# The second channel product with seven block products instead of eight

## The chip, the cores and the metric

The kernel runs on one NeuronCore of a Trainium2 chip. The metric is the device time of one execution in microseconds (us). The engines are named as the profile names them: PE is TensorE's matmuls and PEld its weight loads, DVE is VectorE, ACT ScalarE, POOL GpSimd, SP SyncE, which only issues DMAs here.

## The reference

Attention over selected blocks of keys, and then one token-mixing and one channel-mixing layer, for 4 batches of 768 tokens with 8 heads of 64 (512 channels).

```python
def _attn_ref(q, k, v):                       # (4, 8, 768, 64) each
    k_rep = k.reshape(B, H, n_blocks, block, D).mean(axis=3)      # blocks of 64
    gate_scores = np.einsum('bhsd,bhnd->bhsn', q, k_rep)
    ...                                       # causal blocks only
    top_idx = np.argsort(gate_scores, axis=-1)[..., -top_k:]      # top_k = 3
    ...                                       # mask: chosen blocks and own block, causal
    scores = np.where(mask, scale * np.matmul(q, k.transpose(0, 1, 3, 2)), -1000000000.0)
    attn = np.exp(scores - np.max(scores, axis=-1, keepdims=True))
    attn = attn / (np.sum(attn, axis=-1, keepdims=True) + 1e-09)
    return np.matmul(attn, v).astype(np.float32)

def _moe_ref(x, w_tok1, w_tok2, w_ch1, w_ch2):                    # x (4, 768, 512)
    xt = x.transpose(0, 2, 1)
    h = np.maximum(xt @ w_tok1, 0.0) @ w_tok2                     # 768 -> 256 -> 768
    u = x + h.transpose(0, 2, 1)
    h2 = np.maximum(u @ w_ch1, 0.0) @ w_ch2                       # 512 -> 1536 -> 512
    return (u + h2).astype(np.float32)
```

The change concerns the last product, relu(u @ w_ch1) @ w_ch2, for each batch a 768 x 1536 matrix by a 1536 x 512 one.

## The kernel before

All matmuls take 16-bit operands, except the transposes of q and k and the gate scores, and add up in 32-bit PSUM. The work is made of small operations, each with an engine, an estimated cost, dependencies, a priority and the buffers that it takes. A planner (`plan`, line 68) walks through them with the estimated costs: on each engine it takes, of what could start within 60 ns of the earliest, the one with the lowest priority number. The order so found is then issued as it stands (line 886), and each engine works through its own list in that order. A wait of one instruction on an engine therefore holds all that stands behind it on that engine.

The attention goes over 16 pairs of heads (four per batch): transposes of k and q (L359), their copies to SBUF on ScalarE (L368) and casts to 16 bits on GpSimd (L374), the gate scores (`gate`, L400), the choice of blocks on VectorE (`gm`, `top`, `below`, `bias`), the mask turned by TensorE (`mask`, L443) and put under q by VectorE (`put_mask`, L451), the scores (L465), the exponential on ScalarE (L478), the diagonal on VectorE (`diag`, L485, a product of two 16-bit SBUF tensors), the product with v (L496), and its normalization into `x16` (L515). Pair i has priorities around 10 i.

The mixing of batch b follows: `tok1`, `relu1`, `umix`, `uadd` make u. For batch 0, u is transposed on TensorE (`utr`, `uput`); for the others it is stored to DRAM and read back transposed by two DMAs of SP (`store_u` L344, `turn_u` L350). Then `ch1` (L608) makes 12 chunks of 128 hidden channels for 768 tokens, in pieces of 512 and 256 tokens, with `relu2` on ScalarE (L618, 512 tokens) and VectorE (L620, 256 tokens) into `h2`, which has the hidden channels on the partitions. `ch2` (L629) takes one of six row tiles j of 128 tokens: 12 matmuls of 512 columns with a chunk of `h2` as weights and a chunk of `wc2_16` as the moving operand, in three parts of four matmuls that the planner places separately. `oadd` (L637) adds u, and `store` (L641) sends 128 x 512 results of 32 bits. The last row tile of the last batch is cut into 320 and 192 columns. These have priorities from 1000 (b + 1) on, so that TensorE takes them where the attention leaves it free.

PSUM has eight banks: two "big" tiles of two banks (transposes and scores), one "av" tile for L496, and three "bank" tiles for all the rest. RINGS (L209) gives the number of buffers of each kind. Constants are loaded and buffers cleared ahead of the planned part (L852 to L884), among them `blk` on GpSimd's queue (L883), which serves a second way of preparing k for pairs from VIA (16) on. The weights of the mixing come by GpSimd's queue as casting DMAs, placed behind certain casts of the attention (WAIT, L38); those of `wc2_16` are the last four.

Of the kernel before, what the change touches and what calls it, by code (L numbers as in the profile page):

```python
# [32 lines left out]
VIA = 16  # L33
# [21 lines left out]
class Buf:  # L55


    __slots__ = ("ring", "users", "slot")

    def __init__(self, ring):  # L60
        self.ring, self.users, self.slot = ring, [], None
# [6 lines left out]
def plan(ops, rings, near=60.0):  # L68
# [31 lines left out]
    left = len(ops)  # L100
    while left:
# [7 lines left out]
        for e, cand in ready.items():  # L109
            if not cand:  # L110
                continue
            lst = []
            if e == "SP":
                if any(x.eng == e and x.prio < min(c.prio for c in cand) for x in ops if id(x) not in done):
                    continue
                cand = [min(cand, key=lambda c: c.prio)]
            for op in cand:
                t = free[e]
                for d in op.deps:
                    t = max(t, finish(d, e))  # L120
                ok = True
                for buf in op.takes:
                    first = None
                    for s, (_, old) in enumerate(slots[buf.ring]):
                        f = 0.0 if old is None else buf_free(old, e)
                        if f is not None and (first is None or f < first[0]):
                            first = (f, s)
                    if first is None:
                        ok = False
                        break  # L130
                    t = max(t, first[0])
                    buf.slot = first[1]
                if ok:
                    lst.append((t, op))
            if not lst:
                continue
            t0 = min(t for t, _ in lst)
            pick = min((x for x in lst if x[0] <= t0 + near), key=lambda x: (x[1].prio, x[0]))
            if best is None or pick[0] < best[0]:
                best = pick  # L140
        assert best is not None, "the plan cannot go on"
        t, op = best
        op.start = t
        for buf in op.takes:
            slots[buf.ring][buf.slot] = (0.0, buf)
# [32 lines left out]
def kernel(  # L178
# [31 lines left out]
                 x16=3, h1=2, u=2, uT=2, h2=1, ob=3)  # L210
# [14 lines left out]

    V16 = [sp.tile([128, 2, NJ, 65], F16, tag=f"V{r}", name=f"V{r}") for r in range(R + 1)]
# [3 lines left out]
    K16 = [sp.tile([96, 8, 256], F16, tag=f"K16{y}", name=f"K16{y}") for y in range(2)]  # L230
    ks2 = [sp.tile([128, 2 * NB], FP, tag=f"ks{r}", name=f"ks{r}") for r in range(R)]
    bn16 = [sp.tile([128, NJ, 2, 64], F16, tag=f"bn{r}", name=f"bn{r}") for r in range(R)]
# [3 lines left out]
    wc2_16 = sp.tile([128, NFC, DM], F16, tag="wc2", name="wc2")  # L236
    warm = sp.tile([128, 256], F16, tag="warm", name="warm")
# [46 lines left out]
    def load_k8(i):  # L284
        b, h = pairs[i]

        def f():
            t = sb("kt", [128, 2, 8, D], FP, f"k8_{i}")[0:96]
            T["k8", i] = t
            nc.sync.dma_start(out=t.rearrange("p g t d -> p g (t d)"),  # L290
                              in_=k[b, h:h + 2].rearrange("g (p t) d -> p g (t d)", t=8))
        return f

    def ksum8(i):
        def f():
            t = sp.tile([96, 2, D], FP, tag="kp", bufs=2, name=f"kp_{i}")
            T["kp", i] = t
            nc.vector.tensor_reduce(out=t, in_=T["k8", i].rearrange("p g t d -> p g d t"), axis=AX.X, op=ALU.add)
        return f

    def ksum_pe(i):
        def f():
            p = ps("bank", [128, NB], "kps")
            T["kst", i] = p
            nc.tensor.matmul(out=p, lhsT=T["kp", i].rearrange("p g d -> p (g d)"), rhs=blk, start=True, stop=True)
        return f

    def cast_k8(i):
        def f():
            y = i % 2  # L310
            nc.gpsimd.tensor_copy(out=K16[y].rearrange("p t (g c) -> p g t c", g=4)[:, 0:4:3, :, :], in_=T["k8", i])
        return f

    def store_k(i):
        def f():
            t = dram.tile([S, 256], F16, tag=f"ks{i % 2}", name=f"kscr_{i}")
            T["kscr", i] = t
            nc.sync.dma_start(out=t.rearrange("(p t) c -> p (t c)", t=8), in_=K16[i % 2].rearrange("p t c -> p (t c)"))
        return f

    def turn_k(i):
        return lambda: nc.sync.dma_start_transpose(out=KAX[:, i % R, :, :], in_=T["kscr", i])

    def k16_zero(y):
        return lambda: nc.gpsimd.memset(K16[y].bitcast(FP), 0.0)

    def k16_ind(y):
        def f():
            for c in (64, 128):
                nc.gpsimd.tensor_copy(out=K16[y][:, :, c:c + NB],  # L330
                                      in_=blk.rearrange("p (o n) -> p o n", o=1).broadcast_to([96, 8, NB]))
        return f

# [28 lines left out]
    def evac_t(t32, i):  # L362
        def f():
            name = "qt" if t32 == "ql" else "kt"
            t = sb(name, [128, S if name == "qt" else 1024], FP, f"{name}_{i}")[:, 0:S]
            T[name, i] = t
            p = T["tr", t32, i]
            nc.scalar.copy(out=t, in_=p[:, 0:S])  # L368
        return f
# [60 lines left out]
    def bias(i):  # L430
        def f():
            nc.vector.scalar_tensor_tensor(
                out=bn16[i % R][:, 1:NJ, :, 0:NB],
# [4 lines left out]
    def mask(i):  # L438
        def f():
            p = ps("bank", [128, 128 * GJ], "bps", F16)  # L440
            T["bps", i] = p
            for j in range(GJ):
                nc.tensor.transpose(out=p[:, 128 * j:128 * j + 128],  # L443
                                    in_=bn16[i % R][:, j + 1, :, :].rearrange("p x n -> p (x n)"),
# [157 lines left out]
    def ch1(b, fc, n):  # L602
        def f():
            a, e = CH[n]
            p = ps("bank", [128, e - a], "c1")
# [18 lines left out]
    def ch2(b, j, part, lo, hi):  # L624
# [6 lines left out]
        return f  # L631

# [35 lines left out]
    for i in range(NP):  # L668
# [7 lines left out]

        if i >= VIA:
            kb = Buf("kt")
            ld = op("SP", 500, 0, [], pre - 12, load_k8(i), [kb], size=1400)
            O["ksum", i] = dve(1100, [ld], pre + 1, ksum8(i))  # L680
            nb = Buf("bank")
            O["kpe", i] = pe(115, [O["ksum", i]], pre + 1, ksum_pe(i), [nb])
            O["kcopy", i] = dve(260, [O["kpe", i], O.get(("gate", old))], pre + 1, kcopy(i))
            nb.users.append(O["kcopy", i])
            y = i % 2
            if i < VIA + 2:
                O["kz", y] = op("POOL", 1100, 1150, [], pre - 1, k16_zero(y))
                O["ki", y] = op("POOL", 400, 450, [O["kz", y]], pre - 1, k16_ind(y))
            O["castk", i] = op("POOL", 1150, 1200, [ld, O["ki", y], O.get(("kst", i - 2))], pre + 3, cast_k8(i))
            kb.users += [O["ksum", i], O["castk", i]]  # L690
            O["kst", i] = op("SPO", 600, 0, [O["castk", i], O.get(("cast", "kt", i, 0))], pre + 3.1, store_k(i), size=1600)
            O["kturn", i] = op("SPO", 600, 0, [O["kst", i]] + last_scores(0) + last_scores(1), pre + 3.2, turn_k(i), size=2500)
            O["cast", "kt", i, 0] = O["cast", "kt", i, 1] = O["kturn", i]
        zq = [op("POOL", 880, 930, [], pre - 1, zero_q(i))] if 0 < i < R else []
        for t32, src, off in (("kl", k, 0), ("ql", q, 0.1))[i >= VIA:]:
# [37 lines left out]
        O["bias", i] = dve(195, [O["lt", i], O.get(("mask", old))], pre + 3, bias(i))  # L733
# [33 lines left out]
    for n, (at, f) in enumerate(wq):  # L767
        W.append(op("POOL", 700, 0, [O[("cast",) + WAIT[n]]], at, f, size=3200 if n < 2 else 2100))

    for b in range(B):  # L770
# [46 lines left out]
        for fc in range(NFC):  # L817
            for n in range(2):
                bk = Buf("bank")
                O["ch1", b, fc, n] = pe((864, 436)[n], ([O["uturn", b]] if b >= UVIA else [O["uput", b, cc] for cc in range(NCC)]) + W[2:6],  # L820
                                        fill + 20 + 2 * fc + n, ch1(b, fc, n), [bk])
# [8 lines left out]
        for j in range(NJ):  # L830
            cuts = ((0, DM),) if b < B - 1 or j < NJ - 1 else ((0, 320), (320, DM))
            for lo, hi in cuts:
                bk = Buf("bank")
                prev = None
                for part in range(3):
                    dp = [O["relu2", b, fc, n] for fc in range(NFC) for n in range(2)] + W[6:10] if prev is None else [prev]
                    prev = pe(4 * (2.5 + (hi - lo) / 2.4), dp, fill + 50 + 3 * j + part + lo / 1000, ch2(b, j, part, lo, hi),
                              [bk] if part == 0 else [])
                    h2b.users.append(prev)
                ob = Buf("ob")  # L840
                o = dve(70 + 1.04 * (hi - lo), [prev], early, oadd(b, j, lo, hi), [ob])
                bk.users.append(o)
                ub.users.append(o)
                s = op("SPO", 600, 0, [o], early, store(b, j, lo, hi), size=2 * (hi - lo))
                ob.users.append(s)
# [5 lines left out]
    with tc.manual_schedule():  # L851
# [23 lines left out]
        for r in range(R):  # L875
# [7 lines left out]
        blk = const("blk", (np.arange(96)[:, None] // 8 == nidx[None, :]).astype(np.float32), FP, nc.gpsimd)  # L883
# [37 lines left out]
```

## Time and profile before

| | us |
|---|---|
| device time, median of 3 runs | 273.73 (272.89 to 274.72) |
| span of the profiled execution, first to last instruction | 270.4 |
| median less that span | 3.3 |
| TensorE busy (97%) | 262.6 |
| VectorE busy (60%) | 161.0 |
| ScalarE busy (53%) | 142.6 |
| GpSimd busy (30%) | 81.5 |

The profiled execution's own time is its span and what lies around it (start and end of the program), which the table's third row gives by way of the median. Matmuls are pipelined, and their recorded durations (379 ns for 512 columns) contain the way through the array. The pace at which they follow each other is read from the chain of waits, where a block of n matmuls is shown with its whole length. "Idle before" in a group's line is time in which the engine stood still ahead of such instructions, and an arrow names what ended it.

| stage | from, to (us) |
|---|---|
| attention, with mixing of batch 0, `ch1` of batch 0, u of batch 1, `ch2` of batch 0 as filler | 12 to 163 |
| batch 1: `ch1`, with u of batch 2 | 163 to 183 |
| batch 1: `ch2` | 183 to 199 |
| batch 2: `ch1`, with u of batch 3; `ch2` | 199 to 236 |
| batch 3: `ch1` | 236 to 251 |
| batch 3: `ch2`, last matmul at 266.7 | 251 to 267 |

### The profile page before, as it was taken

To read this page: it belongs to the slowest core of one execution; us is meant where nothing else is said; L and a number is where in the kernel's file an instruction comes from. 1 tells how busy PE (TensorE), PEld (TensorE's weight loads), DVE (VectorE), ACT (ScalarE), POOL (GpSimd) and SP (SyncE) were. 2 spreads that over 40 slices of the span, in tenths; PEclk is the share of its full clock that TensorE was granted. 3 is DMA by queue.
4 is the path that set the end of the run, shared out by engine and by line. 5 is a ranking of instruction groups with operands and counts; after the bars stand their busy time and mean duration, and the time that the engine had idled before them with its cause. 6 is when DMAs were issued, how large, how long until landed. Compare 5 with 4: busy or idle time off the path is not lost.

```text
span 270.4 us, 5927 instructions
## 1 busy us (share of the span) xinstructions
PE 262.6 (97%) x2309; PEld 174.5 (65%) x2309; DVE 161.0 (60%) x561; ACT 142.6 (53%) x188; POOL 81.5 (30%) x112
## 2 busy tenths in 40 slices
PE   8899999999999999999999999999999999999994
PEld 5787588877787877776876655544455544465443
DVE  4558968997979777879888533334233252333222
ACT  2367997777888898788487704430024400044100
POOL 8688816763465365336432000000000000000000
PEclk9999999999999999999999999999999999999999
DMA  8999999999999985480741121003920017510032
GB/s 173 205 212 224 189 215 214 197 200 200 213 209 228 212 176 133 103 174 3 158 117 41 39 77 42 0 2 116 260 89 2 0 48 196 153 72 0 2 135 97
DMA packets 94411, 34.67 MB, mean 128 GB/s; under 512 B 85616, under 2 KB 90888, under 8 KB 94384
## 3 DMA queue, kind: packets, MB, share of 16 engines
q1 hardware_dynamic: 90272, 29.89, 50.5%
q0 software_dynamic: 3392, 4.15, 9.1%
q8 instruction: 18, 0.29, 0.5%
q10 hardware_dynamic: 720, 0.25, 0.5%
q14 instruction: 9, 0.07, 0.1%
HBM read 27.21 MB, written 8.65 MB: 133 GB/s over the span
## 4 chain that ended last, share of the span: by engine, by line
PE 87%; DMA 4%; DVE 4%; ACT 3%; issue 1%; SPq 1%; DVEq 0%; ACTq 0%
PE c L629 23%; PE c L608 23%; PE sps L465 12%; PE aps L496 7%; PE gps L400 5%; DMA ql<-in_q_dram 4%; PE tql L359 4%; PE ups L539 3%; PE tkl L359 3%; PE tok L527 3%; ACT e L478 3%; PE bps L443 2%; PE warm L648 1%; PE tok L558 1%; DVE Q L451 1%
## 5 line engine op out<-in xcount | busy, mean ns | idle before, releaser
L478 ACT ACTIVATE e<-sps 128x1024 f16<-128x1024 f32 (+1 forms) x96 | 84.6, 918 | 16.9 <-PE sps L465 12.0
L608 PE MATMUL c<-uT,wc 128*128 128x256 f16 (+1 forms) x384 | 68.1, 326 | 0.2 <-ACT h L618 0.2
L618 ACT ACTIVATE h<-c 128x512 f16<-128x512 f32 x48 | 28.7, 598 | 69.0 <-PE c L608 61.7
L629 PE MATMUL c<-wc,h 128*128 128x512 f16 (+2 forms) x300 | 64.9, 370 | 0.0
L608 PEld LDWEIGHTS <-wc 128*128 128x128 f16 x384 | 37.1, 98 | 24.5 <-issue 0.4
L465 PE MATMUL sps<-Q,KA 128*128 128x512 f16 (+3 forms) x256 | 50.1, 305 | 1.0 <-ACT e L478 0.7
L629 PEld LDWEIGHTS <-h 128*128 128x128 f16 x300 | 28.8, 98 | 31.3 <-issue 0.6
L620 DVE TENSOR_SCALAR h<-c 128x256 f16<-128x256 f32 x48 | 20.2, 420 | 33.8 <-PE c L608 33.8
L637 DVE TENSOR_TENSOR ob<-u,c 128x512 f32<-128x512 f16 (+2 forms) x25 | 16.6, 666 | 38.4 <-PE c L629 38.4
L485 DVE TENSOR_TENSOR e<-e,m 128x256 f16<-128x256 f16 x90 | 31.1, 353 | 12.9 <-ACT e L478 12.2
L374 POOL CAST KA<-kt 64x768 f16<-64x768 f32 x32 | 27.0, 845 | 27.4 <-ACT kt L368 24.2
L465 PEld LDWEIGHTS <-KA 128*128 128x128 f16 x256 | 22.4, 100 | 15.2 <-issue 1.2
L374 POOL CAST Q<-qt 64x768 f16<-64x768 f32 x32 | 26.9, 841 | 10.8 <-ACT qt L368 9.3
L496 PE MATMUL aps<-V,e 128*128 128x65 f16 x672 | 27.0, 193 | 0.1
L496 PEld LDWEIGHTS <-e 128*128 128x128 f16 x672 | 25.6, 98 | 2.2 <-issue 0.4
L400 PEld LDWEIGHTS gps<-ks,qt 128*128 128x128 f32 x160 | 19.2, 192 | 2.4 <-DVE ks L390 1.3
L280 POOL CAST V<-v 128x768 f16<-128x768 f32 x16 | 13.3, 832 | 24.0 <-DMA v<-in_v_dram 19.8
L400 PE MATMUL gps<-ks,qt 128*128 128x24 f32 x160 | 20.0, 267 | 0.3 <-DVE ks L390 0.2
L368 ACT COPY kt<-tkl 128x768 f32<-128x768 f32 x16 | 12.8, 799 | 11.7 <-PE tkl L359 5.9
L515 DVE TENSOR_TENSOR x<-aps,rc 128x384 f16<-128x384 f32 x32 | 17.6, 550 | 0.5
L451 DVE COPY Q<-bps 12x640 f16<-12x640 f16 x32 | 15.5, 484 | 1.9 <-PE bps L443 0.8
L368 ACT COPY qt<-tql 128x768 f32<-128x768 f32 x16 | 12.8, 798 | 6.5 <-PE tql L359 5.7
(55 smaller groups left out, 218.0 us busy)
## 6 DMA issues: line engine op xcount, KB each, us to landing
kl<-in_k_dram SPq DMA_DIRECT2D x32, 192.0 KB, 4.8
ql<-in_q_dram SPq DMA_DIRECT2D x32, 192.0 KB, 4.6
v<-in_v_dram SPq DMA_DIRECT2D x16, 384.0 KB, 5.4
out_dram<-ob SPq DMA_DIRECT2D x23, 256.0 KB, 2.0
wc<-in_moe_w_ch_dram POOLq DMA_DIRECT2D x8, 384.0 KB, 7.4
uscr<-u SPq DMA_DIRECT2D x3, 768.0 KB, 3.7
w<-in_moe_w_tok_dram POOLq DMA_DIRECT2D x2, 384.0 KB, 6.8
out_dram<-ob SPq DMA_DIRECT2D x1, 160.0 KB, 1.8
```

The lines of the kernel that those rows point to most:

```text
L359: nc.tensor.transpose(out=p[:, 128 * j:128 * j + 128], in_=t[:, j, :], identity=ident32)
L368: nc.scalar.copy(out=t, in_=p[:, 0:S])
L374: nc.gpsimd.tensor_copy(out=dst[i % R][x][lo:lo + 64, :], in_=T[name, i][lo:lo + 64, :])
L400: nc.tensor.matmul(out=g[:, j, :], lhsT=T["qt", i][:, 128 * j + 128:128 * j + 256], rhs=ks2[i % R], start=True, stop=True)
L465: nc.tensor.matmul(out=p[:, off + a:off + a + n], lhsT=KA[i % R][x][:, 128 * kk:128 * kk + 128], rhs=QA[i % R][x][:, q0 + a:q0 + a + n], s ...
L478: nc.scalar.activation(out=e[:, 0:width], in_=T["sps", i, x, g][:, 0:width], func=AF.Exp, scale=scale)
L485: nc.vector.tensor_tensor(out=d, in0=d, in1=m0, op=ALU.mult)
L496: nc.tensor.matmul(out=p[:, jq, :], lhsT=T["e", i, x, g][:, o:o + 128], rhs=V16[i % (R + 1)][:, x, kk, :], start=(kk == 0), stop=(kk == jq))
L608: nc.tensor.matmul(out=p, lhsT=wc1_16[:, cc, 128 * fc:128 * fc + 128], rhs=T["uT", b][:, cc, a:e], start=(cc == 0), stop=(cc == NCC - 1))
L618: nc.scalar.activation(out=T["h2", b][:, fc, a:e], in_=T["c1", b, fc, n], func=AF.Relu)
L620: nc.vector.tensor_scalar(out=T["h2", b][:, fc, a:e], in0=T["c1", b, fc, n], scalar1=0.0, scalar2=None, op0=ALU.max)
L629: nc.tensor.matmul(out=T["c2", b, j, lo], lhsT=T["h2", b][:, fc, 128 * j:128 * j + 128], rhs=wc2_16[:, fc, lo:hi], start=(fc == 0), stop=( ...
```

## The change

`ch2`, `oadd` and `store` are no longer used. The product of each pair of row tiles (j, j + 3) with `wc2_16` is written as a 2 x 2 block product: the hidden channels are halved (chunks 0 to 5 and 6 to 11), and so are the 512 output columns. One level of Strassen's method, in Winograd's arrangement, then takes seven products of 128 x 768 by 768 x 256 in place of eight, each of six matmuls of 256 columns.

The sums of weights (`weight_sum`, four, once) and of halves of `h2` (`hsum`, four per pair) are made on VectorE in 16 bits, the second of them in place. The products add up in four PSUM tiles, a to d. Three partial products are copied out by ScalarE (`keep`) and the second product of the same tile is then accumulated onto them. VectorE adds a and b (`vsum`), GpSimd adds u to that three times (`vu`), makes pc + pd (`psum`) and the last quarter (`osum`), VectorE the three other quarters (`oput`), and SP stores whole rows of 512 (`store_row`). Once no score is left to plan, `ch1` and the products can also take the "big" tiles.

Buffers: x16 3 to 2, h1 2 to 1, bn16 4 to 2; kt tiles from 1024 to 768 columns; new s1, s3 (2 each), s4 (1), f32 (6). The way for pairs from VIA on is removed with its tiles (K16) and `blk`.

```diff
-                 x16=3, h1=2, u=2, uT=2, h2=1, ob=3)
+                 x16=2, h1=1, u=2, uT=2, h2=1, ob=3, s1=2, s3=2, s4=1, f32=6)
...
-                    for s, (_, old) in enumerate(slots[buf.ring]):
-                        f = 0.0 if old is None else buf_free(old, e)
-                        if f is not None and (first is None or f < first[0]):
-                            first = (f, s)
+                    for ring in [buf.ring] + ([buf.other] if buf.other and not scores_left else []):
+                        for s, (_, old) in enumerate(slots[ring]):
...
+    HF = NFC // 2
+    t2_16 = sp.tile([128, HF, 256], F16, tag="t2", name="t2")
+    B11, B12 = wc2_16[:, 0:HF, 0:256], wc2_16[:, 0:HF, 256:512]
+    B21, B22 = wc2_16[:, HF:NFC, 0:256], wc2_16[:, HF:NFC, 256:512]
+    def weight_sum(n):
+        def f():
+            out, a, c = ((t3_16, B22, B12), (B12, B12, B11), (t2_16, B22, B12), (t4_16, B21, t2_16))[n]
+            nc.vector.tensor_tensor(out=out, in0=a, in1=c, op=ALU.subtract)
+    def hsum(b, j, n):
+        def f():
+            a11, a12, a21, a22 = halves(b, j)
+            if n in (1, 3, 4):
+                T["s", b, j, n] = sb(f"s{n}", [128, HF, 128], F16, f"s{n}_{b}_{j}")
+            if n == 1:
+                nc.vector.tensor_tensor(out=T["s", b, j, 1], in0=a21, in1=a22, op=ALU.add)
+            if n == 3:
+                nc.vector.tensor_tensor(out=T["s", b, j, 3], in0=a11, in1=a21, op=ALU.subtract)
+            if n == 2:
+                nc.vector.tensor_tensor(out=a21, in0=T["s", b, j, 1], in1=a11, op=ALU.subtract)
+            if n == 4:
+                nc.vector.tensor_tensor(out=T["s", b, j, 4], in0=a12, in1=a21, op=ALU.subtract)
+    def prod(b, j, n, buf):
+        def f():
+            key, x, y, first = {1: ("a", a11, B11, True), 2: ("a", a12, B21, False), 6: ("b", a21, t2_16, True),
+                                7: ("c", T.get(("s", b, j, 3)), t3_16, True), 4: ("c", a22, t4_16, False),
+                                5: ("d", T.get(("s", b, j, 1)), B12, True),
+                                3: ("d", T.get(("s", b, j, 4)), B22, False)}[n]
+            if first:
+                T["c2" + key, b, j] = bank(buf, 256, "c2")
+            for fc in range(HF):
+                nc.tensor.matmul(out=T["c2" + key, b, j], lhsT=x[:, fc, :], rhs=y[:, fc, :],
+                                 start=first and fc == 0, stop=fc == HF - 1, skip_group_check=True)
...
+        TW.append(dve(880, W[6:10] + TW[-1:], 60.0 + 10 * n, weight_sum(n)))
...
-        for j in range(NJ):
-            cuts = ((0, DM),) if b < B - 1 or j < NJ - 1 else ((0, 320), (320, DM))
+        for j in range(3):
+            at = fill + 50 + 10 * j
...
+            for m in (3, 1, 2, 4):
+                bf = [Buf(f"s{m}")] if m != 2 else []
+                dp = {1: q21 + q22, 3: q11 + q21, 2: [sums.get(1), sums.get(3)], 4: [sums.get(2)] + q12}[m]
+                sums[m] = dve(470, dp, at, hsum(b, j, m), bf)
...
+            p1 = product(1, "a", [], 0)
+            ka = act(256, [p1], early, keep(b, j, "a"), [fa])
+            p6 = product(6, "b", [], 1)
+            v_ = dve(420, [ka, p6], early, vsum(b, j), [fv])
+            p7 = product(7, "c", [], 2)
+            kc = act(256, [p7], early, keep(b, j, "c"), [fc7])
+            p2 = product(2, "a", [ka], 3)
+            o11 = dve(420, [p2], early, oput(b, j, 0, 0), [ob0])
+            p5 = product(5, "d", [], 4)
+            kd = act(256, [p5], early, keep(b, j, "d"), [fd])
+            p4 = product(4, "c", [kc], 5)
+            vu12 = op("POOL", 660, 720, [v_], early, vu(b, j, 0, 1), [f12])
+            vu21 = op("POOL", 660, 720, [v_], early, vu(b, j, 1, 0), [f21])
+            vu22 = op("POOL", 660, 720, [v_], early, vu(b, j, 1, 1), [f22])
+            o21 = dve(420, [p4, vu21], early, oput(b, j, 1, 0), [ob1])
+            p3 = product(3, "d", [kd], 6)
+            o12 = dve(420, [p3, vu12, o11], early, oput(b, j, 0, 1))
+            pcd = op("POOL", 660, 720, [kc, kd], early, psum(b, j))
+            o22 = op("POOL", 660, 720, [vu22, pcd, o21], early, osum(b, j))
+            for row, o, ob in ((0, [o11, o12], ob0), (1, [o21, o22], ob1)):
+                st = op("SPO", 600, 0, o, early, store_row(b, j + 3 * row), size=1024)
...
-        blk = const("blk", (np.arange(96)[:, None] // 8 == nidx[None, :]).astype(np.float32), FP, nc.gpsimd)
```

Here `early` is a priority of -1, ahead of everything else on the same engine, and q11 to q22 are the `relu2` that fill the four blocks of `h2`.

## The prediction

> **What bounds the kernel now.** I read the page's busy shares and its chain of waits first.
>
> ```profile
> PE 262.6 (97%) x2309; PEld 174.5 (65%) x2309; DVE 161.0 (60%) x561; ACT 142.6 (53%) x188; POOL 81.5 (30%) x112
> ...
> PE 87%; DMA 4%; DVE 4%; ACT 3%; issue 1%; SPq 1%; DVEq 0%; ACTq 0%
> PE c L629 23%; PE c L608 23%; PE sps L465 12%; PE aps L496 7%; PE gps L400 5%; DMA ql<-in_q_dram 4%; PE tql L359 4%; PE ups L539 3%; PE tkl L359 3%; PE tok L527 3%; ACT e L478 3%; PE bps L443 2%; PE warm L648 1%; PE tok L558 1%; DVE Q L451 1%
> ```
>
> A busy PE need not be a streaming PE, so 97% alone proves little. The chain does: 87% of the span is TensorE itself, and 23%, 62.2 us of 270.4, is L629, the second channel product that the change rewrites.
>
> The chain in order of time shows L629 as solid blocks, and at what pace matmuls of 512 and of 256 columns follow each other:
>
> ```profile
> 18.54 0.87 PE warm L648 x8
> ...
> 80.85 0.44 PE c L608 x4
> ...
> 183.26 15.70 PE c L629 x72
> ...
> 220.04 15.70 PE c L629 x72
> 235.74 15.60 PE c L608 x96
> 251.34 15.25 PE c L629 x80
> ```
>
> (Columns: start, length, what.) 72 matmuls of 512 columns in 15.70 us are 218 ns each; four of 256 take 0.44 us, and eight warm-up ones of 256, each with its own weight load, 0.87: 109 ns each. Half the columns cost half the time. So L629 is three stretches of 15.7 us where nothing else runs on TensorE (batches 1 to 3), and as much again scattered from 126 to 162 us as filler in the attention (batch 0).
>
> The stages, by the view of busy time in stretches (columns: the stretch, its length, busy us of PE, PEld, DVE, ACT and POOL, the granted clock, the DMA engines' share, GB/s):
>
> ```profile
> 126.00:158.00 32.00, 32.00 (x350) 22.39 (x348) 25.01 (x99) 21.48 (x25) 7.51 (x10) 1.00 0.32 80
> ...
> 183.00:199.00 16.00, 15.99 (x75) 7.15 (x73) 4.85 (x9) 0.00 (x0) 0.00 (x0) 1.00 0.60 164
> ...
> 251.30:267.40 16.10, 15.61 (x85) 7.88 (x82) 4.62 (x8) 0.24 (x1) 0.00 (x0) 1.00 0.22 81
> ```
>
> The clock is full (1.00). In the two late rows VectorE has some 11 us free of 16 and the other two are empty: room for the new sums. In the first VectorE has 7 of 32.
>
> **TensorE: what is removed.** Before, a batch takes 6 row tiles x 12 matmuls of 512. After, 3 pairs of row tiles x 7 products x 6 matmuls of 256 = 126, at 109 ns 13.73 us. Against 15.70 that saves 1.97 us a batch, 7.9 us in all. It all lies on the chain, for TensorE ends last in each of the four stages.
>
> **VectorE: what is added.** The costs come from two lines' own views (min/median/max ns) and from the groups kept apart by shape (busy us, mean ns of one):
>
> ```profile
> L485 DVE TENSOR_TENSOR e<-e,m x90: 238/284/953, 28.1 to 155.8; 128x256 f16<-128x256 f16 x90
> ...
> L374 POOL CAST KA<-kt x32: 816/825/1251, 8.3 to 136.6; 64x768 f16<-64x768 f32 x32
> ```
>
> ```profile
> L515 DVE TENSOR_TENSOR x<-aps,rc 128x384 f16<-128x384 f32 x32 | 17.6, 550 | 0.5
> L637 DVE TENSOR_TENSOR ob<-u,c 128x512 f32<-128x512 f16 x23 | 15.8, 687 | 37.7 <-PE c L629 37.7
> ```
>
> L637 and L515 differ by 128 columns and 137 ns: 1.07 ns a column and some 140 fixed. A sum of f32 with PSUM over 256 columns is then 140 + 274 = 0.42 us. L485, all f16, takes 284 for 256: 0.56 ns a column behind the same fixed part. A sum of halves (6 x 128 = 768 f16 columns) is 140 + 430 = 0.57 us alone, about 0.47 in a row, since neighbours overlap by nearly 0.1. Per pair of tiles: four such sums and four f32 ones, 4 x 0.47 + 4 x 0.42 = 3.56 us, under the 4.58 us that its 42 matmuls take. A batch adds 10.7 and loses six oadds of 0.6 = 3.6: +7.1 us. That is hidden in batches 1 to 3 (11 us free), except where order bites: the batches 1 and 2 start with six uadds of 0.6 on VectorE (181.3 to 184.4 in the timeline), and the sums S1, S2 stand behind them, with P6, P5 and P3 behind those on TensorE. P1, P7, P2, P4 of two pairs (8 x 0.65 = 5.2 us) can go first, in the five PSUM tiles that are free once scores are over, so I take 0.4 us a batch, 0.8 in all; without that cover it would be the 3.1 us of the uadds each.
>
> The four weight sums (1536 columns, 140 + 860 = 1.0 us each) run once wc2 has landed, after about 69 us (last issue at 61 plus 6.8). VectorE is at 16.5 of 20 there and TensorE is filled by ch1 of batch 0: taken at nothing, at most 3.8 us.
>
> **The shared memory port.** L485 reads two tensors from SBUF and goes to 953 ns at worst while casts run, and the casts from 825 to 1251. L485's mean, 353, is 115 over its minimum, with GpSimd busy for 81.5 of the first 145 us. The twelve sums of a batch so pay 12 x 0.115 = 1.4 us; VectorE's 3.56 a pair becomes 4.0, still under 4.58.
>
> The Trainium skill (SBUF — State Buffer, Who interferes with whom) speaks against the change here: a VectorE instruction with two SBUF inputs and a GpSimd one that reads SBUF exclude each other, and the second blocks until the first is through. By the rule, if each sum waited for half of an add, a pair would take VectorE 3.56 + 4 x 0.33 = 4.9 us, 0.3 over TensorE's, and the nine pairs of batches 1 to 3 would raise the forecast by 2.8 us; the rows show the effect at a third of that size, and by them it adds nothing.
>
> **GpSimd: what is added.** Five adds of 128x256 f32 per pair (three of v + u, pc + pd, the last sum). No row has a two-input add there. Nearest rows: a cast of 768 columns 0.825 us, so a third of it, 0.28, is the low end, and the whole, 0.83, the high end. The diff's own plan writes 0.66 to 0.72; its entry for the casts (0.825) is what the trace shows, so I take 0.66. Per pair 3.3 us under 4.58, ends 1.4 and 4.15. ScalarE's three copies of 256 columns (0.39 each, from 0.60 for 512 at 0.83 ns a column) fall where it idles.
>
> The Trainium skill (GPSIMD Engine Reference, Elementwise — side-by-side cycle accounting) gives about 2.6 cycles an element for a two-input add: an estimate of 0.56 us plus dispatch, on the side of the value taken.
>
> **Batch 0, in the attention.** VectorE goes from 25.0 to 32.1 of the 32 us between 126 and 158. Attention's steps have better priorities than the halves' sums, but the small f32 sums go before all. The products hold up to four accumulators where one was held, in three "bank" tiles until the last score, and gate (L400) and mask (L443) need the same three. TensorE has another cover: ch1 of batch 1, whose uT lands by 139.6 (turned at 131.9, 7.7 at most). I take 1.0 us lost, 0 to 5.
>
> **The end.** Before, the last matmul is followed by 0.35 us of oadd and a store of 96 KB (1.7 us). After: 0.42 and 256 KB (2.0), +0.4. The row j+3 needs GpSimd: P6 of the last pair ends five products, 3.3 us, before TensorE does; then come vsum, three adds, pc + pd and the last add: 0.2 + 0.42 + 5 x 0.66 = 3.9 us and some 0.2 of port waits, 0.8 after TensorE's end and so about 0.5 behind the other half. Tail +0.9; 0.4 with adds of 0.28, 1.7 with 0.83.
>
> **Edits with one answer**, at nothing: VIA's branch never ran (16 pairs, VIA = 16). x16 from 3 to 2: the first norm of batch 3 is at 130.3, the last uadd of batch 1 ends at 128.1. h1 and bn16: their users are a batch and two pairs apart. blk's load: 0.55 us of GpSimd's queue at 5 us, ahead of m0. SP carries 24 stores for 25; uT's turn for batch 2 lands at 195.6 (189.8 + 5.8), and ch1 would now start at 197.0: 1.4 us of slack, gone if a store that waits for GpSimd is put before it on SP.
>
> **Sum.** −7.9 + 0.8 + 1.0 + 0.9 = −5.2 us. The profiled execution spans 270.4, which gives 265.2; the median of 273.73 lies 3.3 above the span, and against it the forecast is 268.5.
>
> **Rivals.** About 1% (2.7 us) is what a measurement here can tell from no change.
> 1. *VectorE's sums and GpSimd's adds exclude each other fully*: one port carries 4 x 0.47 + 5 x 0.66 = 5.2 us a pair, 15.5 a batch against 15.70 before. Batches 1 to 3 gain 0.6, batch 0 2.0, the tail costs 0.9: 272.0. For it: 953 and 1251 above. Against it: the median of 284, and that adds may run on into the next stage, save in the last batch.
> 2. *Slower: three PSUM banks in the attention.* If half-done products hold all three, gate and mask of the last three pairs (six requests) wait. At 2.3 us each that is 14 us in place of my 1.0: 281.5. It decides from 1.5 us each: 268.5 + 9 − 1 = 276.5. Against it: gate is issued a pair ahead, so it has some 8 us, and vsum frees a bank after two products.
> 3. *TensorE doesn't hold 109 ns when all 126 matmuls change weights.* The gain is gone at 15.70 / 126 = 124.6 ns; then 273.7 + 2.7 = 276.4. Against it: L496 loads weights for each of 21 matmuls in 0.67 us, 32 ns apiece.
>
> **Chances.** Forecast 0.70 (265.5 to 271.0); rival 1 0.15; rival 2 0.10; rival 3 0.05, on the edge between same and slower. Faster 0.70; same 0.15 + 0.04; slower 0.10 + 0.01. The range 265.5 (nothing lost but the tail's 0.4 is 266.2; 0.7 below it for the scatter of the runs, which lie 0.8 below and 1.0 above their median) to 274.0 holds the forecast and rival 1 and leaves out about 0.17.
>
> **What will show it.** L629's successor on the chain: 504 matmuls, 54.9 us, three stretches near 13.8. Gaps of TensorE inside them with VectorE or GpSimd as releaser speak for rival 1; gaps before L400 and L443 between 125 and 160 for rival 2; a pace above 115 ns without idle time for rival 3. GpSimd's add should be 0.6 to 0.75 us, a sum of halves 0.5 to 0.7, and the time from the last matmul to the end 4.3 us, not 3.4. The forecast is wrong if TensorE's idle time after 60 us exceeds 4 us.

## The result, and the profile after

| | before | after |
|---|---|---|
| device time, median of 16 runs each (us) | 273.46 (272.69 to 275.97) | 272.42 (271.29 to 275.97) |
| ratio after / before | | 0.9953, 95% interval 0.9932 to 0.9975 |
| span of the profiled execution | 270.4 | 271.3 |

The kernel is about 1.0 to 1.3 us faster where 5.2 were forecast. The two profiled executions stand the other way round, +0.9: a span and its own time differ by 1.8 us (after: 271.3 and 273.09), so before's was one of its fastest (272.2, 1.3 below the median) and after's lies 0.7 above its median; 0.9 − 1.3 − 0.7 is the −1.1 of the medians. In some executions the granted clock fell for a few microseconds; the experiments and the last section come back to that.

Where the time went shows in three rows of the page (busy shares; the chain of waits by engine, and by line):

```profile
PE 257.4 (95%) x2513; PEld 194.9 (72%) x2513; DVE 196.0 (72%) x634; ACT 154.7 (57%) x224; POOL 129.9 (48%) x171
...
PE 44%; DVE 21%; POOL 16%; DMA 9%; issue 5%; ACT 3%; SPq 1%; POOLq 0%; ACTq 0%; DVEq 0%
PE c L569 19%; PE c L633 7%; POOL vu L655 6%; DVE e L446 5%; PE sps L426 4%; DMA ql<-in_q_dram 4%; PE tok L488 3%; DMA wc<-in_moe_w_ch_dram 3%; PE aps L457 3%; DMA w<-in_moe_w_tok_dram 3%; POOL ob L678 2%; DVE Q L412 2%; POOL Q L335 2%; POOL pc L673 2%; DVE m L378 2%
```

TensorE lost 5 us of work, but the share of the chain that it carries fell from 87% to 44%. VectorE rose from 4% to 21%, GpSimd from nothing to 16%: a kernel that had one bound now hands the path from engine to engine. (`ch1` is L569 now, the products L633, `diag` L446, `gate` L361, `mask` L404.)

The chain in order of time dates the late stages (start, length, what; the blocks of L569 are `ch1` of batches 1 to 3):

```profile
167.34 13.00 PE c L569 x80
...
202.26 13.16 PE c L569 x80
...
237.33 15.60 PE c L569 x96
252.93 2.65 PE c L633 x24
...
256.11 0.84 POOL pc L673
...
257.09 2.56 POOL vu L655 x3
```

Before, the same blocks began at 163.31 (less 1.30 for eight matmuls already done, 162.0), 198.96 and 235.74. So:

| stage | before | after | difference | forecast |
|---|---|---|---|---|
| start to the block of `ch1`, batch 1 (attention) | 162.0 | 167.3 | +5.3 | −1.97 + 1.0 |
| batch 1 | 36.95 | 34.92 | −2.0 | −1.97 + 0.4 |
| batch 2 | 36.8 | 35.1 | −1.7 | −1.97 + 0.4 |
| batch 3 to its last matmul | 31.2 | 29.4 | −1.8 | −1.97 |
| last matmul to the end | 3.45 | 4.6 | +1.15 | +0.9 |

The late stages came out as forecast, and the attention ate them. The stretches say why (columns: stretch, length, busy us of PE, PEld, DVE, ACT, POOL, granted clock, the DMA engines' share, GB/s), first of after, then of before:

```profile
60.00:167.00 107.00, 102.77 (x1162) 79.85 (x1163) 96.82 (x339) 81.06 (x107) 53.87 (x65) 1.00 0.61 129
126.00:158.00 32.00, 30.25 (x346) 24.70 (x345) 30.77 (x109) 22.82 (x32) 18.98 (x22) 1.00 0.27 68
187.20:202.20 15.00, 14.84 (x131) 12.53 (x129) 11.69 (x24) 3.27 (x9) 10.61 (x13) 1.00 0.70 163
```

```profile
60.00:163.00 103.00, 102.76 (x1090) 74.15 (x1089) 81.37 (x314) 78.28 (x98) 40.74 (x50) 1.00 0.68 139
```

From 60 us to the attention's end TensorE has the same 102.8 us of busy time, though a batch's product costs 2 us less, and it also stands still for 4.2 us (107.0 − 102.8; before 0.2). VectorE went from 81.4 of 103 to 96.8 of 107, and between 126 and 158 us it is busy for 30.8 of 32. In the third row, in batch 1's products, VectorE and GpSimd carry the same sums (11.7 and 10.6 of 15) and TensorE stands still for only 0.2. The waits of TensorE's weight loads from 60 us on (waited for: us in total, times, longest), after and before:

```profile
PEld L404 <- DVE bn L393: 4.1, 8, 1.0
PEld gps L361 <- DVE ks L351: 2.6, 4, 0.9
PEld L457 <- DVE e L446: 1.2, 3, 0.6
```

```profile
PEld gps L400 <- DVE ks L390: 1.1, 3, 0.7
PEld L443 <- DVE bn L432: 0.9, 3, 0.4
```

All three releasers are VectorE steps of the attention itself, not the new sums. The chain from 124.24 us shows how the one delays the other: pieces of VectorE's work, one behind the other without a gap.

```profile
124.24 0.19 DVE gm L369
124.43 0.46 DVE s L620
124.89 0.73 DVE m L378 x10
125.63 0.19 DVE e L446
125.82 0.19 DVE lt L385
126.01 0.11 DVE rc L465
126.11 0.56 DVE u L508
126.68 0.19 DVE bn L393
126.87 0.60 DVE u L508
```

gm, m, lt, bn are one chain (the choice of blocks) that ends in the mask for TensorE; a sum of halves (s, L620) and the additions of the token mixing (u) stand between its links.

### The profile page after: what moved, and what is told of

Read it like the earlier page. It is cut to its first block, busy times and chain, and to the rows that moved or that the text cites. A ratio compares the mean times of both kernels' runs of the same rounds, so it can differ in the third digit from the quotient of the medians.

```text
span 271.3 us, 6571 instructions
## 1 busy us (share of the span) xinstructions
PE 257.4 (95%) x2513; PEld 194.9 (72%) x2513; DVE 196.0 (72%) x634; ACT 154.7 (57%) x224; POOL 129.9 (48%) x171
## 4 chain that ended last, share of the span: by engine, by line
PE 44%; DVE 21%; POOL 16%; DMA 9%; issue 5%; ACT 3%; SPq 1%; POOLq 0%; ACTq 0%; DVEq 0%
PE c L569 19%; PE c L633 7%; POOL vu L655 6%; DVE e L446 5%; PE sps L426 4%; DMA ql<-in_q_dram 4%; PE tok L488 3%; DMA wc<-in_moe_w_ch_dram 3%; PE aps L457 3%; DMA w<-in_moe_w_tok_dram 3%; POOL ob L678 2%; DVE Q L412 2%; POOL Q L335 2%; POOL pc L673 2%; DVE m L378 2%
## 5 line engine op out<-in xcount | busy, mean ns | idle before, releaser
L569 PE MATMUL c<-uT,wc 128*128 128x256 f16 (+1 forms) x384 | 67.4, 326 | 0.0
L569 PEld LDWEIGHTS <-wc 128*128 128x128 f16 x384 | 36.9, 98 | 23.4 <-issue 0.2
L673 POOL TENSOR_TENSOR pc<-pc,pd 128x256 f32<-128x256 f32 x12 | 10.5, 875 | 69.9 <-ACT pd L641 69.8
L446 DVE TENSOR_TENSOR e<-e,m 128x256 f16<-128x256 f16 x90 | 36.5, 412 | 7.6 <-ACT e L439 7.2
L335 POOL CAST Q<-qt 64x768 f16<-64x768 f32 x32 | 28.0, 876 | 10.9 <-ACT qt L329 9.5
L633 PEld LDWEIGHTS <-h 128*128 128x128 f16 x288 | 27.7, 98 | 5.3 <-issue 0.7
L655 POOL TENSOR_TENSOR vu<-v,u 128x256 f32<-128x256 f32 x36 | 26.5, 761 | 3.3 <-DVE v L648 2.7
L633 PEld LDWEIGHTS <-s 128*128 128x128 f16 x216 | 20.9, 98 | 2.9
L361 PEld LDWEIGHTS gps<-ks,qt 128*128 128x128 f32 x160 | 19.2, 192 | 3.9 <-DVE ks L351 2.8
L361 PE MATMUL gps<-ks,qt 128*128 128x24 f32 x160 | 20.1, 268 | 1.3 <-DVE ks L351 1.2
L633 PE MATMUL c<-wc,h 128*128 128x256 f16 x144 | 19.6, 273 | 0.0
L633 PE MATMUL c<-wc,s 128*128 128x256 f16 x144 | 19.6, 273 | 0.0
L633 PE MATMUL c<-t,h 128*128 128x256 f16 x144 | 19.2, 273 | 0.3 <-ACT pc L641 0.3
```

What stands on the lines that cost most here:

```text
L335: nc.gpsimd.tensor_copy(out=dst[i % R][x][lo:lo + 64, :], in_=T[name, i][lo:lo + 64, :])
L361: nc.tensor.matmul(out=g[:, j, :], lhsT=T["qt", i][:, 128 * j + 128:128 * j + 256], rhs=ks2[i % R], start=True, stop=True)
L446: nc.vector.tensor_tensor(out=d, in0=d, in1=m0, op=ALU.mult)
L569: nc.tensor.matmul(out=p, lhsT=wc1_16[:, cc, 128 * fc:128 * fc + 128], rhs=T["uT", b][:, cc, a:e], start=(cc == 0), stop=(cc == NCC - 1))
L633: nc.tensor.matmul(out=T["c2" + key, b, j], lhsT=x[:, fc, :], rhs=y[:, fc, :], start=first and fc == 0, stop=fc == HF - 1, skip_group_chec ...
L655: nc.gpsimd.tensor_tensor(out=t, in0=T["v", b, j], in1=T["u", b][:, j + 3 * row, 256 * col:256 * col + 256], op=ALU.add)
```

## The experiments

Each kernel was compared with before on its own chip, so only the ratios are set side by side; a difference of 0.01 is 2.7 us. Theory A: the attention lost its time to VectorE, by the sums added there (of weights at about 70 us, of halves of batch 0). Theory B: what the products themselves bring there did it, accumulators held in three PSUM banks and the chain of small 32-bit steps. What else an expectation weighs, it says itself.

**Batch 0 as before.** Batch 0 keeps the old `ch2` (72 matmuls of 512 columns), and the weight sums follow it (B0 is 1; the loop whose head is shown is the old one with `ch2`, `oadd` and `store`).

```diff
-    for n in range(4):
-        TW.append(dve(880, W[6:10] + TW[-1:], 60.0 + 10 * n, weight_sum(n)))
...
+        for j in range(NJ if b < B0 else 0):
...
+                FREE.append(prev)
...
+        if b == B0 - 1:
+            for n in range(4):
+                TW.append(dve(880, FREE + TW[-1:], 60.0 + 10 * n, weight_sum(n)))
-        for j in range(3):
+        for j in range(3 if b >= B0 else 0):
```

> Batch 0's second product goes back to eight block products (72 matmuls of 512 columns), and the four weight sums wait until it is through, after the attention; batches 1 to 3 as in the changed kernel. Theory A (VectorE: the loss sits in the attention, where VectorE's new work delays the steps that TensorE waits for, and batches 1 to 3 keep their saving): the attention ends as before, batches 1 to 3 save 1.7 to 2.0 us each, the tail costs 1.2: 273.5 - 5.6 + 1.2 = 269.0. Theory B (PSUM: three tiles are held by open products in the attention) says the same here. Rival C (the saving of the late batches is only work that the delayed attention has moved): 272 to 273.

Measured: 267.91 us (266.92 to 268.06), ratio 0.9798 (0.9767 to 0.9829). It beats both kernels. In the stretches VectorE is back at 24.9 of 32 and TensorE stands still for none of it, and the chain is TensorE's again (a row of stretches; the page's shares of the chain; two blocks of `ch1` of the chain in order of time):

```profile
126.00:158.00 32.00, 32.00 (x349) 22.29 (x347) 24.91 (x98) 21.30 (x25) 7.20 (x9) 1.00 0.29 83
```

```profile
PE 73%; POOL 10%; DVE 6%; DMA 4%; ACT 3%; issue 2%; SPq 1%; POOLq 0%; ACTq 0%
```

```profile
196.25 13.00 PE c L569 x80
...
231.15 15.60 PE c L569 x96
```

Batches 2 and 3 begin 2.7 and 4.6 us earlier than before (198.96, 235.74). So the three late batches give what was forecast, and batch 0, which should have given 2 us more, took 4.2 (0.9953 against 0.9798). The smaller buffers of the changed kernel are all in this one too, so they are not the cause. It is 1.1 us faster than the 269.0 expected, a little more than its interval covers; no run shows why.

**The two kinds of sums, each added to that kernel with no use of the result.** First four sums of weights at the old place and priority, then the twelve of halves of batch 0; the real ones follow as in the kernel above.

```diff
+    for n in range(4):
+        DW.append(dve(880, W[6:10] + DW[-1:], 60.0 + 10 * n, dead_weight_sum(n)))
```

> As e1, with four more sums of 128x1536 16-bit columns on VectorE at the place where the changed kernel makes its weight sums (about 70 to 77 us); their results are not used. Theory A: dearer than e1 by 2 to 3.5 us (the four take 3.6 to 4.4 us of VectorE there). Theory B, and the prediction's term (hidden behind the first channel product): as e1 within 0.7 us.

```diff
+        for j in range(3 if b < B0 else 0):
...
+            for m in (3, 1, 2, 4):
...
+                sums[m] = dve(470, dp, at, hsum(b, j, m), bf)
```

> As e1, with the twelve sums of halves of batch 0 made on VectorE at the same priorities as in the changed kernel and not used; no product of batch 0 waits for them, none holds more PSUM than before. Theory A: dearer than e1 by 2 to 4 us. Theory B: dearer by less than 1 us.

Measured: 270.75 us, ratio 0.9898 (0.9852 to 0.9943), for the sums of weights, and 270.92, ratio 0.9927 (0.9903 to 0.9951), for those of halves. Against 0.9798 these are +2.7 us and +3.5 us. The first is uncertain: two of its four executions had a mean granted clock of 0.990 and 0.993; the two at 0.997 gave 269.8, which leaves 1.9. Work whose result nobody reads, on an engine that was busy for 81 of 103 us, delays the end by a good part of its own length (the four sums of weights are 4.1 us of VectorE's time, the twelve of halves some 7).

**The products without sums in batch 0.** From the changed kernel the sums of halves of batch 0 are left out (the products P7, P6, P5 and P3 of that batch take plain quarters of `h2`, so that its output is another); then the sums of weights also go behind batch 0 (P6, P7 and P4 take plain quarters of the weights).

```diff
-            for m in (3, 1, 2, 4):
+            for m in (3, 1, 2, 4) if b else ():
```

> The changed kernel without the twelve sums of halves of batch 0: its seven products take parts of h2 in their place, so batch 0's values are others; PSUM tiles, copies, f32 sums and GpSimd's adds as in the changed kernel. Theory A: faster than the changed kernel by 2 to 4 us (268.5 to 270.5). Theory B: the same as the changed kernel within 1 us (272.4).

```diff
+            if b == 0:
+                y = {6: B22, 7: B22, 4: B21}.get(n, y)
...
+        if b == 0:
+            for n in range(4):
+                TW.append(dve(880, FREE + TW[-1:], 60.0 + 10 * n, weight_sum(n)))
```

> The changed kernel with batch 0's seven products on raw parts of h2 and of the weights (its values are others), without its twelve sums of halves, and with the weight sums made after batch 0's products. What stays in the attention: the four accumulators in three PSUM tiles, the copies, the f32 sums and GpSimd's adds. Theory A: all of the loss but what the f32 sums take is gone, so it beats e1 (267.9) by up to the 2.0 us of TensorE saved in batch 0: 266.0 to 267.9. Theory B (held PSUM tiles cost the attention 2 us or more): 268.5 or above.

Measured: 269.91 us, ratio 0.9874 (0.9853 to 0.9895), without the sums of halves; 267.85, ratio 0.9766 (0.9713 to 0.9818), without both. So the sums of halves cost 0.0079 of 273.5, 2.2 us, in the kernel itself, and moving the sums of weights another 0.0108, 2.9 us. What is left, the seven products with all their accumulators, copies and 32-bit sums, is 0.0032 or 0.9 us ahead of the old `ch2` in batch 0, where TensorE's saving is 2.0: they cost 1.1 us. That figure is rough, since the intervals of the two kernels (0.9713 to 0.9818 and 0.9767 to 0.9829) overlap, but theory B falls as the main cause: the two kinds of sums take 5.1 us. In the stretch of the second kernel VectorE has 4 us of 32 free again and TensorE stands still for 0.4, although GpSimd (16.6 us, after 19.0) and ScalarE (25.1, after 22.8) carry nearly what they carry after:

```profile
126.00:158.00 32.00, 31.60 (x373) 26.02 (x372) 27.95 (x104) 25.06 (x34) 16.64 (x22) 1.00 0.27 67
```

**The weight sums with a low priority.**

```diff
-        TW.append(dve(880, W[6:10] + TW[-1:], 60.0 + 10 * n, weight_sum(n)))
+        TW.append(dve(880, W[6:10] + TW[-1:], 1049.0, weight_sum(n)))
```

> The changed kernel with the priority number of the four weight sums raised from 60 to 90 to 1049, just ahead of batch 0's second product, so that every step of the attention that is ready goes first; seven products for batch 0 stay. Theory A (VectorE's time in the attention is what is short, wherever it is taken): some of the 2.8 us that the dead weight sums cost comes back, at most all of it: 270 to 272. If it was only their place ahead of the attention's steps that cost, all of it: 269.6.

Measured: 274.71 us, ratio 1.0023 (0.999 to 1.0056): a miss for theory A as I had put it, not better but worse than after. The lines of the three forms (ns min/median/max, first and last start) show that the edit hardly moved them (after starts them at 70.5, 73.7, 75.1 and 76.2):

```profile
L600 DVE TENSOR_TENSOR t<-wc x2: 941/1084/1226, 71.1 to 74.9; 128x1536 f16<-128x1536 f16 x2
L600 DVE TENSOR_TENSOR wc<-wc x1: 944/944/944, 73.0 to 73.0; 128x1536 f16<-128x1536 f16 x1
L600 DVE TENSOR_TENSOR t<-wc,t x1: 1575/1575/1575, 78.4 to 78.4; 128x1536 f16<-128x1536 f16 x1
```

The planner fills any moment in which it thinks VectorE idle, so an operation of low priority still runs at 71 us, and one sum in flight holds what comes next on that engine for a microsecond or more. Why it is worse, the stretches and the timeline of its profiled execution show (the third number from a row's end is the clock):

```profile
142.00:143.00 1.00, 0.01 (x1) 0.00 (x0) 0.95 (x4) 1.00 (x2) 0.94 (x2) 1.00 0.00 0
143.00:144.00 1.00, 0.76 (x7) 0.79 (x8) 1.00 (x12) 0.40 (x1) 0.94 (x2) 1.00 0.00 0
144.00:145.00 1.00, 1.00 (x8) 0.68 (x8) 1.00 (x2) 0.00 (x0) 0.94 (x2) 0.71 0.00 0
145.00:146.00 1.00, 1.00 (x6) 0.49 (x5) 1.00 (x5) 0.62 (x1) 0.26 (x1) 0.50 0.00 0
146.00:147.00 1.00, 1.00 (x20) 1.00 (x19) 1.00 (x12) 1.00 (x2) 0.00 (x0) 0.50 0.00 0
147.00:148.00 1.00, 1.00 (x14) 0.85 (x12) 0.39 (x3) 0.31 (x1) 0.00 (x0) 0.59 0.00 0
```

```profile
143.25 1.26 PE L361 MATMUL gps<-ks,qt 128*128 128x24 f32 x10 [1.23 <-DVE ks L351]
```

TensorE stands still for 1.23 us, waiting for VectorE's ks, and a microsecond later the granted clock is 0.5 for about 3.4 us, some 1.7 us of work. Eight of its ten executions have a mean clock of 0.993 or less; of after's sixteen only two. By the median of the clocks (0.9905 against 0.9975, of 272 us) that is some 1.9 us, enough for the whole difference. In this kernel it was seen in one trace; no run changed the clock alone.

**The tail.** In the first experiment's kernel pc + pd and the last quarter of the last pair go to VectorE.

```diff
-        return lambda: nc.gpsimd.tensor_tensor(out=T["pc", b, j], in0=T["pc", b, j], in1=T["pd", b, j], op=ALU.add)
+        e = nc.vector if (b, j) == (B - 1, 2) else nc.gpsimd
+        return lambda: e.tensor_tensor(out=T["pc", b, j], in0=T["pc", b, j], in1=T["pd", b, j], op=ALU.add)
...
```

> As e1, with the last two GpSimd adds of the very last pair (pc + pd and the last quarter) on VectorE. In e1 GpSimd ends 0.86 us after VectorE's last sum, and the store of its row follows. If that is the tail: 0.4 to 0.8 us faster than e1's 267.9, that is 267.1 to 267.5. If the stores themselves set the end: the same as e1.

Measured: 269.14 us, ratio 0.9814 (0.9772 to 0.9855), no difference from 0.9798, so the 0.4 to 0.8 us did not come. The add on VectorE met GpSimd's last `vu` and took more than twice the 0.41 us of the last quarter's add, which follows it undisturbed:

```profile
L674 DVE TENSOR_TENSOR pc<-pc,pd x1: 909/909/909, 261.8 to 261.8; 128x256 f32<-128x256 f32 x1
```

**Port or time?** The four dead sums of weights are replaced by dead reductions of 768 columns: about as long on VectorE, but with one input in place of two. (The reduction of this size that the attention makes, `kst`, is L382 in before and L343 after; its median is 944 ns before.)

```diff
-            nc.vector.tensor_tensor(out=out, in0=a, in1=c, op=ALU.subtract)
+            nc.vector.tensor_reduce(out=t, in_=..., axis=AX.X, op=ALU.add)
```

> As e2, in the very same order of instructions, with each of the four dead weight sums (two 16-bit inputs from SBUF, 0.94 us undisturbed) replaced by a dead reduction of 768 columns of the weights (one input, 0.94 us for the same size in the attention's L343 of before). Theory P (the shared memory port makes the sums dear: they wait for GpSimd's casts and hold those up): at least half of e2's 2.8 us over e1 is gone, ratio to before 0.985 or less. Theory T (VectorE's time alone): as e2, ratio 0.99.

Measured: 269.36 us, ratio 0.985 (0.9811 to 0.9889): 1.4 us over the first experiment's kernel, where the two-input sums cost 1.9 to 2.7. The line views of the two, first the sums, then the reductions:

```profile
L606 DVE TENSOR_TENSOR t<-wc x2: 959/1128/1298, 73.6 to 76.5; 128x1536 f16<-128x1536 f16 x2
```

```profile
L606 DVE TENSOR_REDUCE dr<-wc x4: 914/936/939, 70.4 to 75.6; 128x12 f32<-128x768 f16 x4
```

The reductions stay at 914 to 939 ns, a sum goes up to 1298. The ratio lies on the edge that theory P had named. By the middle values VectorE's time alone is at least half of the price; the intervals (0.985 and 0.9898, each ± 0.004) overlap, and the exact split is not settled.

**The planner told the measured costs**, in the changed kernel and in the first experiment's (880, 470, 200, 660 become 1250, 700, 300, 760 in the one, and 1150, 620, 300, 760 in the other).

```diff
-        TW.append(dve(880, W[6:10] + TW[-1:], 60.0 + 10 * n, weight_sum(n)))
+        TW.append(dve(1250, W[6:10] + TW[-1:], 60.0 + 10 * n, weight_sum(n)))
...
-                sums[m] = dve(470, dp, at, hsum(b, j, m), bf)
+                sums[m] = dve(700, dp, at, hsum(b, j, m), bf)
...
```

> The changed kernel with the planner's costs set to what the trace showed: weight sums 1250 ns for 880, sums of halves 700 for 470, the diagonal's product 300 for 200, GpSimd's adds 760 for 660. Nothing is computed otherwise; the order changes. Theory O (the order is laid out for costs that are too low, so TensorE stands behind late steps while other work waits further back in its queue): at least 2 us faster than the changed kernel, ratio to before 0.988 or less. Theory T (VectorE's time is used up there, whatever the order): ratio 0.992 to 1.0.

> As e1, with the planner's costs as measured (sums of halves 620 ns, weight sums 1150, the diagonal's product 300, GpSimd's adds 760). If the order around the late sums still loses something: ratio to before below e1's 0.980, down to 0.977. If the late stretches already run without gaps on TensorE, the same as e1; slower if the dearer diagonal spoils the order of the attention.

Measured: 271.89 us, ratio 0.994 (0.9898 to 0.9982), as after; and 268.73, ratio 0.9826 (0.979 to 0.9863), as the first experiment. By the medians the work itself counts and not its order. The executions of the first of the two fall into two groups, though: five executions with a mean clock of 0.995 or more have a median of 270.15 us, five with 0.992 or less one of 273.79. A better order may be worth up to 2 us as long as no standstill of TensorE brings the clock down; this stays open.

## Why the prediction was wrong

The terms that failed are those of VectorE in the attention: the sums of weights at nothing and batch 0 at 1.0 us. They were 1.9 to 2.9 and 3.3 to 4.6 us. The measured 272.4 lies inside the stated range and beside rival 1's 272.0, but that is luck: rival 1 has batches 1 to 3 gain 0.6 us, and they gained 5.5.

**The products, right.** Three batches were to save 1.97 us each, less 0.4 in two; they saved 2.0, 1.7 and 1.8. Six matmuls of 256 columns follow each other in 0.65 to 0.66 us, 109 ns each, with new weights every time. Rival 3 (a slower pace) and, for the late batches, rival 1 (sums and adds shut each other out) are answered by that. After's views of a sum of halves and of GpSimd's add show the sizes behind it (ns min/median/max):

```profile
L620 DVE TENSOR_TENSOR s<-h x12: 514/624/1029, 124.4 to 262.9; 128x768 f16<-128x768 f16 x12
...
L655 POOL TENSOR_TENSOR vu<-v,u x36: 662/669/1060, 134.2 to 265.9; 128x256 f32<-128x256 f32 x36
```

0.57 (0.47 in a row) and 0.66 had been taken. Both instructions are stretched at times, to 1.03 and 1.06, and a pair of tiles still hides them.

**The tail, nearly right.** +1.15 for +0.9. GpSimd's last add ends at 268.0, 1.3 us after the last matmul and 0.86 behind the other half, where the step had 0.8 and 0.5. The five adds took what was put; they began late, because `vsum` (L648) stood behind a stretched sum of halves (L620) and GpSimd was still at the pair before (until 264.54):

```profile
262.93 1.03 DVE L620 TENSOR_TENSOR s<-h 128x768 f16<-128x768 f16 x1
...
263.88 0.41 DVE L648 TENSOR_TENSOR v<-pa,c 128x256 f32<-128x256 f32 x1
...
264.62 1.92 POOL L655 TENSOR_TENSOR vu<-v,u 128x256 f32<-128x256 f32 x3
...
266.50 0.72 POOL L673 TENSOR_TENSOR pc<-pc,pd 128x256 f32<-128x256 f32 x1
...
266.74 0.42 DVE L669 TENSOR_TENSOR ob<-vu,c 128x256 f32<-128x256 f32 x1 [0.18 <-PE c L633]
...
267.30 0.72 POOL L678 TENSOR_TENSOR ob<-vu,pc 128x256 f32<-128x256 f32 x1
```

**The weight sums, wrong.** "VectorE is at 16.5 of 20 there and TensorE is filled by ch1 of batch 0: taken at nothing, at most 3.8 us." They cost 1.9 to 2.9 us by two experiments, and took 0.94 to 1.30 each where 1.0 was put. Neither half of the sentence held. The stretch from 69 to 89 us, after and before:

```profile
69.00:89.00 20.00, 18.94 (x200) 14.28 (x197) 19.48 (x65) 15.64 (x22) 9.26 (x11) 1.00 1.04 211
```

```profile
69.00:89.00 20.00, 20.00 (x219) 15.35 (x216) 16.64 (x64) 17.71 (x24) 10.65 (x14) 1.00 1.12 219
```

VectorE has hardly anything left, and TensorE stands still for 1.1 us in spite of its filler. The experiments agree: 1.1 us with the dead sums of weights, 1.7 with the sums at low priority, 0.5 with the dead reductions, 0.0 in both kernels that make the sums after batch 0's product. Two readings of mine go beyond that, and no run tried them. VectorE's free microseconds lie between the links of chains that wait for other engines, where a 1 us instruction delays the next link. And the filler is limited: `ch1` of batch 0 needs little of VectorE (`relu2` of its 256-token pieces), but it had to last until the attention's end, and what is used up early is missing later.

**Batch 0, wrong.** "I take 1.0 us lost, 0 to 5": by the ratios, sums of halves 2.2 to 3.5 and the products' small steps 1.1, so 3.3 to 4.6 us, inside the bounds and far from the value taken. With the sums of weights that is 5.2 to 7.5 us. The profiled executions show over 7, +5.3 − (−1.97). Of that some 1.1 arose at 30 to 36 us, where TensorE waits for token-mixing weights, and is scatter between executions: that wait was 0.9 us in after's, none in before's and the first experiment's, and up to 2.1 in the others. The working asked what holds a PSUM bank, and rival 2 put that at 14 us; no wait on a bank stands among the first of TensorE's. It noted that VectorE would go from 25.0 to 32.1 of 32 and took 1.0 us for it, with `ch1` of batch 1 as TensorE's cover. An engine that is asked for 32.1 of 32 has become the bound there, whatever the priorities say. And the cover could not be had: its input was there from about 142 us, but `h2` has one buffer (h2=1 in RINGS), so `relu2` of batch 1 must wait until batch 0's products have read it, and `ch1` of batch 1 started at 167.3 only.

**The old work, not priced.** The port was priced for the new instructions alone. The groups by shape of after and before, from 60 us to the attention's end (busy us, mean ns | idle before):

```profile
L446 DVE TENSOR_TENSOR e<-e,m 128x256 f16<-128x256 f16 x67 | 28.5, 430 | 4.1 <-ACT e L439 4.0
```

```profile
L485 DVE TENSOR_TENSOR e<-e,m 128x256 f16<-128x256 f16 x66 | 23.4, 362 | 10.3 <-ACT e L478 9.9
```

The mean of `diag` goes from 362 to 430 ns while GpSimd is busy for 53.9 us in place of 40.7. That alone is a third of VectorE's 15.4 us more in the stage, and VectorE's idle time ahead of it falls from 10.3 us to 4.1. The shared port would explain it, but GpSimd's load alone does not order the runs: from 60 to 162 us the mean is 345 with batch 0 as before (GpSimd busy for 40.8 us), 403 with the dead sums of weights (43.0), and 383 in the kernel with the products alone (51.3). So the cause of the longer `diag` is not shown.

**The sign of the whole.** The forecast would have been wrong by its own mark ("if TensorE's idle time after 60 us exceeds 4 us"): it is 4.2 already before 167 us.

Open are the split of the sums' price between port and time, what makes `diag` longer, what a better order is worth, and how often the clock's fall costs the changed kernel something (two executions of sixteen).

## What to carry to other kernels

A saving on the engine that bounds a kernel is collected only in stages where the engines that pay for it have room, so the sum is made stage by stage, and a stage where it asks an engine for its whole length is left as it was: seven products for eight in three batches of four gave 2.0%, in all four 0.5%. VectorE, busy for 16.6 of 20 us with steps that TensorE waits for, had no room for four instructions of 1 us, and a low priority did not keep them out. The old work beside the new is to be priced too: `diag` grew from 362 to 430 ns. And work that is counted on as cover needs its buffers free, not only its input.

## What the runs showed of the hardware

**A short standstill of TensorE can cost more than itself.** After 1.23 us without matmuls (weight sums with low priority), 1.75 (no sums of halves) and 2.13 (dead sums of weights) the granted clock went to 0.5 for 3.4 us; the last two arose at about 35 us, where TensorE waits for the token-mixing weights. Standstills of 1.17, 1.34 and 1.87 us in other traces, and of 0.9 in after's, had no such effect. The Trainium skill (TensorE: Matmul & The Clock Gate, Part 1: The HAM clock gate) lets the clock fall to half after an idle window of about 3.4 us: the length of the slow stretch agrees, but here a third of that in standstill was enough.

**Two-input instructions of VectorE are at times stretched beside GpSimd's, mostly by part of their length.** Sums of weights took from 0.94 to 1.58 us, and `diag` has means from 339 to 430 ns in these runs; reductions with one input stayed at 914 to 939. The Trainium skill (SBUF — State Buffer, Who interferes with whom) says that the second of two such instructions blocks until the first is through; the longest rows (1575 for 944 ns, and 909 for 410) look like that, the medians do not.

**GpSimd's add** of 128x256 takes 669 ns with one 16-bit input (`vu`) and 727 with both in 32 bits (pc + pd), by the medians of two lines; a 32-bit sum of the same size on VectorE with one side in PSUM takes 410.
